# Moving four filter loads from SyncE's queue to GpSimd's

## The chip, the cores and the metric

The kernel runs on one core of a Trainium2 chip. The metric is the device time of one execution in microseconds; lower is better. A profile of one execution shows, beside its time, the span from the first to the last instruction and what every engine did in it: PE (TensorE matmuls; PEld is its weight loads), DVE (VectorE), ACT (ScalarE), POOL (GpSimd) and SP (SyncE, which here only issues transfers).

## What is computed

The input x is bf16, one sequence of 2048 positions with 512 channels. Two blocks follow each other, each with a residual.

```
x  = A_x                                              # 1 x 2048 x 512, bf16
h  = x + irfft2( rfft2(layernorm(x)) * (w_r + i*w_i) )  # over positions and channels
z  = layernorm(layernorm(h))                          # the second block normalizes twice
u  = gelu( einsum("bsd,sf->bdf", z, w1) + b1 )        # mixes positions, f = 1376
h2 = h + transpose( einsum("bdf,fs->bds", u, w2) + b2 )
```

w_r and w_i are 2048 x 257, bf16: the filter, a complex factor for every frequency. w1 is 2048 x 1376 and w2 is 1376 x 2048.

## The kernel before

**The Fourier transforms are matmuls with constant matrices.** The 2048 positions are split as 128 times 16, so a transform over positions is one stage of 128-point matrices (`A`, 16 of them, with the matrix F already scaled by each row's 1/standard deviation) and one of 16-point matrices (`C`). The 512 channels are transformed between them (`B`). After the filter the same comes back: `I`, `Bi` and `Ai`. The code keeps 16 chunks c of the spectrum, each holding two values of tau (2c and 2c + 1).

**One chunk's way through the middle of the kernel** is short, and the prediction follows it by these names:

- `B{c}` on PE, `Be{c}` empties its PSUM bank into a buffer (ACT or DVE);
- `C{c}` on PE, `Ce{c}` empties it into Xsb (a p behind the number means two chunks in one step);
- `P{c}` on DVE multiplies the spectrum by the filter: a tensor_tensor of Xsb and the tile W (line 674);
- `I{c}` on PE transforms back, `Ie{c}` empties it into TT (lines 708 and 709). `I{c}` uses PSUM bank 5 + c mod 3, so I10 needs the bank that Ie7 empties.

After the last chunk come `ID`, `Bi`, `Ai` (the rest of the inverse transform and the residual), the second block's norm, `m1` (line 844, matmul with w1), gelu (line 944) and `m2` (lines 962 and 968, matmul with w2), and the stores.

**Where the filter comes from.** The tile W holds 32 values of tau, for w_r (comp 0) and w_i (comp 1). It is loaded in three pieces of tau (line 510):

```
pieces = [(0, 8), (8, 18), (18, 32)]
```

Piece 0 serves P0 to P3, piece 1 P4 to P8, piece 2 P9 to P15. A load fills every fourth partition (32 of 128) with rows of 256 bf16 values, 512 bytes each, so piece 2 is eight loads of 32 x 14 rows, 224 KB each: four of w_r, then four of w_i. All loads of a piece count on one semaphore, and a P waits for the whole piece.

**The order of work.** A small planner, `schedule`, orders the instructions of each engine; for PE, ACT, DVE and POOL the beginning of the order is a list written out by hand, passed in `K.schedule`. SP has no list: it issues by the loads' `prio`, which is x and F first, then E, L and H, then W piece 0, 1 and 2 (`prio` 1.0, 2.0 and 3.0), then ID, GD and IF, then w1 and w2. `gen_sync` turns dependences into semaphore waits, and an engine runs its list strictly in order.

DVE's list in the stretch at hand is

```
P4 Be8 P5 Ie2_0 P7 P6 Ie4_0 P9 P8 Ie6_0 P10 P11 Ie7_0 P13 P12 Ie10_0 P14 P15 Ie14_0 Ie15_0
```

and PE's is

```
I4 B13 B12 C10p I6 I5 B14 C12p I7 B15 I8 I9 C14 I10 C15 I11 I12 I13 I14 I15 wmd ID00
```

POOL multiplies F by the row scales (`fs0` to `fs15`, line 577), then computes seven small vectors of negated means (`nm`, line 617, first read after the last chunk), then issues three small loads of the two bias vectors (`ld_b1a`, `ld_b2`, `ld_b1b`), each behind a wait for `Ye15`, the last emptying of stage A, and casts them to fp32 (lines 937 to 940).

Of the kernel before, what the change touches and what calls it, by code (L numbers as in the profile page):

```python
# [11 lines left out]
NP = 128  # L12
# [453 lines left out]
def build_kernel(nc, A_x, A_w_r, A_w_i, B_w1, B_b1, B_w2, B_b2, out, verbose=False):  # L466
# [10 lines left out]
    X, Y, FS, F, E, Lm, Hm, W, TT, GD, IF = (T[n] for n in ("X", "Y", "FS", "F", "E", "Lm", "Hm", "W", "TT", "GD", "IF"))  # L477
# [9 lines left out]
    def dma(name, q, dst, src, nbytes, prio=0.0, after=(), group=None, wgroup=None, store=False, land=None):  # L487
        def emit(e, eng):
            with nc.allow_non_contiguous_dma(reason="layout"):
                return eng.dma_start(dst, src)  # L490
        return K.op(name, q, emit, ins=[src] if store else [], outs=[] if store else [dst], occ=450.0, prio=prio,
                    after=after, nbytes=nbytes, group=group, wgroup=wgroup, land=land)
# [18 lines left out]
    for pi, (ta, tb) in enumerate(pieces):  # L511
        for comp, wsrc in enumerate((A_w_r, A_w_i)):
            wv = wsrc.rearrange("(q r) k -> q r k", r=64)
            for reim in range(2):
                parts = [(0, ta, tb, wv[:, ta:tb, 1:257])]
                lo = ta
                if ta == 0:
                    parts.append((1, 0, 1, wv[:, 32:33, 1:257]))
                    lo = 1
                parts.append((1, lo, tb, wv[:, 64 - lo:64 - tb:-1, 1:257]))  # L520
                for ss, a, b, src in parts:
                    dma(f"ld_w{comp}_{pi}_{reim}_{ss}_{a}", "sp", W[2 * ss + reim:NP:4, a:b, comp, :], src, 32 * 512 * (b - a),
                        prio=1.0 + pi, group=f"W{pi}", wgroup=f"W{pi}")

    K.op("mk_eps", "dve", lambda e, eng: eng.memset(eps[:, 0:1], LN_EPS), outs=[eps[:, 0:1]], occ=70.0, lat=130.0, prio=0)  # L525
    K.op("mk_eps2", "dve", lambda e, eng: eng.memset(eps[:, 1:2], LN_EPS * LN_EPS), outs=[eps[:, 1:2]], occ=70.0, lat=130.0, prio=0)
# [21 lines left out]
    for ga, gb in RS_GROUPS:  # L548
# [18 lines left out]
        for n2 in range(ga, gb):  # L567
            if n2 < NSPLIT:
                for sg in range(2):
# [4 lines left out]
                         prio=-5 + 0.1 * g)  # L574
# [380 lines left out]
    for n2 in range(NS2):  # L955
        b = 3 + n2 % 5
# [14 lines left out]
        else:  # L971
# [19 lines left out]
               "ag14 bn15 ag15 Ye6 Ye10 Ye14 Be2 Ce0 P0 P1 Ie0_0 P3 P2 Be7 P4 Be8 P5 Ie2_0 P7 P6 Ie4_0 P9 P8 Ie6_0 P10 P11 Ie7_0 P13 P12 "  # L991
               "Ie10_0 P14 P15 Ie14_0 Ie15_0 Bie01 bq01 bq00 aq0 sd2_1 sd2_0 hh00 hh01 h01 h00 hh1 h2 sd3_0 sd3_1 sd4_0 sd4_1 h3 sd5_1 hh2 "
               "sd5_0 h4 sd6_1 sd6_0 hh3 h5 sd7_1 hh4 h6 sd8_0 sd7_0 hh5 sd8_1 h7 sd9_1 hh6 sd9_0 h8 hh7 sd10_1 sd10_0 h9 hh8".split(),
        "pool": "fs1 fs0 fs2 fs4 fs5 fs3 fs6 fs7 fs8 fs9 fs12 fs10 fs11 fs13 fs14 fs15 nm2 nm7 nm3 nm4 nm0 nm1 nm8 ld_b1a ld_b2 ld_b1b b2f "
               "b1f_a b1f_b".split(),
    })
    K.gen_sync()
# [31 lines left out]
def bass_sequential_preLN__spectral_gfnet__mixer_token_mlp__prompt_kernel(  # L1029
    nc,  # L1030
    A_x,
    A_w_r,
    A_w_i,
    B_x,
    B_w1,
    B_b1,
    B_w2,
    B_b2,
    out,
):  # L1040
    build_kernel(nc, A_x, A_w_r, A_w_i, B_w1, B_b1, B_w2, B_b2, out)
# [28 lines left out]
```

## Time and profile before

| | |
|---|---|
| median of 7 runs | 130.81 us (130.15 to 132.22) |
| the profiled execution | 130.81 us, span 129.0 us |
| TensorE clock granted | 1.00 |
| busy: PE, DVE, ACT, POOL | 121.4, 65.1, 65.0, 11.8 us |
| read from HBM, written | 20.49 MB, 2.10 MB |

Busy time is the time in which an engine executes instructions; issuing a transfer is not counted in it, so SP has none. In timelines a line gives start and length in microseconds, the engine (SPq is SP's sequencer), the line of the kernel, the operation, what it writes and reads, and how many instructions are merged; in square brackets stands the idle time of the engine before it and who ended it. Instructions on one engine overlap a little: DVE's casts last 0.69 us each but follow each other every 0.61 us. Times of a view are counted from the start of the span.

### The profile page before, as it was taken

What the parts mean: (1) busy time and instruction counts of PE and PEld (TensorE: products, weight loads), DVE (VectorE), ACT (ScalarE), POOL (GpSimd) and SP (SyncE); (2) the same over time, 40 slices, a digit from 0 to 9 for tenths busy, and PEclk for the clock granted to TensorE, in tenths of its full rate; (3) what the DMA queues carried; (4) which work ended last, traced back from release to release, by engine and by line L of the source; (5) the groups of instructions that cost most, each with busy time, mean ns of one, the idle gap of its engine ahead of it and who ended that gap; (6) DMA issues with size and microseconds to landing.
All of it is one profiled execution on the core that took longest, in us unless ns stands there. A gap on an engine that the chain in (4) does not pass through costs nothing.

```text
span 129.0 us, 2036 instructions
## 1 busy us (share of the span) xinstructions
PE 121.4 (94%) x777; PEld 74.1 (57%) x786; DVE 65.1 (50%) x141; ACT 65.0 (50%) x137; POOL 11.8 (9%) x33
## 2 busy tenths in 40 slices
PE   6959979999899999999999999999999999999990
PEld 2337657777676655555544444456666666666660
DVE  1689949986978999968650000000422423323322
ACT  4688979999868999897777712222000000000000
POOL 0058980200000000000000000000000000000000
PEclk9999999999999999999999999999999999999999
DMA  3999998999999999999100000000112111121121
GB/s 71 371 395 380 242 219 169 277 319 363 396 425 425 415 416 422 244 390 400 42 0 0 0 0 5 0 0 0 41 49 73 41 67 60 41 81 41 41 84 41
DMA packets 16505, 22.71 MB, mean 176 GB/s; under 512 B 1552, under 2 KB 12304, under 8 KB 16368
## 3 DMA queue, kind: packets, MB, share of 16 engines
q1 hardware_dynamic: 15808, 21.66, 48.5%
q10 hardware_dynamic: 576, 0.92, 2.0%
q8 instruction: 6, 0.10, 0.3%
q0 software_dynamic: 112, 0.01, 0.3%
q14 instruction: 3, 0.02, 0.1%
HBM read 20.49 MB, written 2.10 MB: 175 GB/s over the span
## 4 chain that ended last, share of the span: by engine, by line
PE 71%; SPq 18%; DVE 3%; DMA 3%; issue 2%; DVEq 0%
PE ps L844 29%; PE ps L962 28%; SPq L490 18%; PE ps L771 5%; DMA W<-in_A_w_i_dram 3%; PE ps L692 3%; PE ps L808 2%; DVE P L674 2%; PE ps L968 2%; PE ps L911 1%; DVE TT L709 1%; DVE OUT L974 1%; PE ps L864 0%; PE ps L801 0%; PE ps L533 0%
## 5 line engine op out<-in xcount | busy, mean ns | idle before, releaser
L844 PE MATMUL ps<-HH,W 128*128 128x512 bf16 (+1 forms) x168 | 39.4, 379 | 0.2
L962 PE MATMUL ps<-GT,W 128*128 128x512 bf16 (+1 forms) x162 | 35.7, 379 | 0.2
L974 DVE SCALAR_TENSOR_TENSOR OUT<-ps,B2f,H 128x512 bf16<-128x512 f32 x16 | 12.0, 751 | 46.7 <-PE ps L962 24.4
L962 PEld LDWEIGHTS ps<-GT,W 128*128 128x128 bf16 (+1 forms) x165 | 23.7, 144 | 12.0
L844 PEld LDWEIGHTS ps<-HH,W 128*128 128x128 bf16 (+1 forms) x170 | 16.9, 100 | 17.6 <-issue 0.2
L944 ACT ACTIVATE GT<-ps,B1f 128x512 bf16<-128x512 f32 (+1 forms) x11 | 7.0, 691 | 12.7 <-PE ps L844 11.8
L818 DVE TENSOR_TENSOR H<-ps,X 128x512 bf16<-128x512 f32 x14 | 9.7, 691 | 4.0 <-PE ps L808 3.4
L824 ACT ACTIVATE SQ<-H,nm 128x512 bf16<-128x512 bf16 x14 | 10.1, 721 | 2.7 <-DVE H L818 2.4
L674 DVE TENSOR_TENSOR P<-Xsb,W 128x1024 bf16<-128x1024 bf16 x16 | 10.4, 685 | 1.6 <-DMA W<-in_A_w_i_dram 1.5
L559 DVE BATCH_NORM_STATS2 st<-X 128x6 f32<-128x512 bf16 x13 | 8.3, 679 | 3.6 <-DMA X<-in_A_x_dram 3.5
L593 PE MATMUL ps<-FS,X 128*128 128x256 bf16 x64 | 8.0, 273 | 1.7 <-POOL FS L577 1.6
L692 PE MATMUL ps<-Hm,P 128*128 128x128 bf16 x128 | 9.1, 220 | 0.5 <-DVE TT L709 0.4
L781 ACT ACTIVATE EO<-ps 128x512 bf16<-128x512 f32 x15 | 8.8, 586 | 0.9 <-PE ps L771 0.7
L637 PE MATMUL ps<-E,Y 128*128 128x256 bf16 x64 | 8.5, 273 | 0.7 <-ACT Y L607 0.7
L771 PE MATMUL ps<-GD,TT 128*128 128x256 bf16 x60 | 9.0, 273 | 0.1
L692 PEld LDWEIGHTS ps<-Hm,P 128*128 128x128 bf16 x128 | 7.4, 98 | 2.5 <-issue 1.3
L665 ACT ACTIVATE Xsb<-ps 128x1024 bf16<-128x1024 f32 (+1 forms) x9 | 8.0, 886 | 0.5 <-PE ps L652 0.4
L577 POOL TENSOR_SCALAR FS<-F,rs 128x256 bf16<-128x256 bf16 x16 | 7.4, 481 | 7.7 <-DMA F<-c_F 6.5
L641 ACT ACTIVATE Bsb<-ps 128x512 bf16<-128x512 f32 x13 | 7.3, 594 | 1.2 <-PE ps L637 1.2
L593 PEld LDWEIGHTS ps<-FS,X 128*128 128x128 bf16 x64 | 5.3, 97 | 4.5 <-POOL FS L577 3.0
L771 PEld LDWEIGHTS ps<-GD,TT 128*128 128x128 bf16 x60 | 5.8, 98 | 3.0 <-ACT EO L781 0.2
L533 PE MATMUL ps<-WM 128*128 128x512 bf16 (+1 forms) x19 | 6.2, 475 | 1.2 <-DVE eps L525 1.2
(70 smaller groups left out, 96.3 us busy)
## 6 DMA issues: line engine op xcount, KB each, us to landing
W<-in_B_w_dram SPq DMA_DIRECT2D x8, 688.0 KB, 11.7
W<-in_B_w_dram SPq DMA_DIRECT2D x10, 512.0 KB, 17.8
out_dram<-OUT SPq DMA_DIRECT2D x16, 128.0 KB, 1.7
X<-in_A_x_dram SPq DMA_DIRECT2D x4, 256.0 KB, 6.4
F<-c_F SPq DMA_DIRECT2D x4, 256.0 KB, 6.5
IF<-c_IF SPq DMA_DIRECT2D x1, 1024.0 KB, 7.2
W<-in_A_w_r_dram SPq DMA_DIRECT2D x4, 224.0 KB, 3.6
W<-in_A_w_i_dram SPq DMA_DIRECT2D x4, 224.0 KB, 3.8
```

Source lines behind the costliest of these rows:

```text
L490: return eng.dma_start(dst, src)
L593: r = eng.matmul(ps[:, b, 256 * u:256 * u + 256].rearrange("p (a b) -> p a b", a=2), X[:, n2, 128 * t:128 * t + 128], fr if t < 2 else fa, ...
L637: r = eng.matmul(o, Y[:, k, c, :], E[:, k, :].rearrange("p (h r) -> p h r", h=2), start=(i == 0), stop=(i == 3), skip_group_check=True)
L674: return eng.tensor_tensor(P[:, :, :, :], x.unsqueeze(2).broadcast_to([NP, 2, 2, 256]), W[:, 2 * c:2 * c + 2, :, :], ALU.mult)
L692: r = eng.matmul(o, P[:, h, m, par::2], Hm[:, v, m, :].rearrange("p (m r) -> p m r", r=4), start=(h == 0 and m == 0 and (par == 0 or b != ...
L771: r = eng.matmul(o, TT[:, q, n2, par, :], GD[:, par, q, :], start=(i == 0), stop=(i == 3), skip_group_check=True)
L781: return eng.activation(eo[:, :], ps[:, bE, :], ACT.Copy)
L818: K.op(f"h{n2}", "dve", lambda e, eng: eng.tensor_tensor(H[:, n2, :], ps[:, bA, :], X[:, n2, :], ALU.add), ins=[ps[:, bA, :], X[:, n2, :]] ...
L824: K.op(f"sq{n2}", "act", lambda e, eng: eng.activation(sq[:, :], hsrc, ACT.Square, bias=nm[:, n2, 0:1], accum_out=s2t[:, n2, 0:1]), ins=[h ...
L844: return eng.matmul(ps[0:Mt, bank, :], W1[:, n2, 128 * t:128 * t + Mt], HH[:, n2, :], start=(n2 == 0), stop=(n2 == 15), skip_group_check=True)
L962: r = eng.matmul(ps[:, b, :], W2[t][0:Kt, n2::16], GT[0:Kt, t, :], start=(t == 0), stop=(t == NFT - 1), skip_group_check=True)
L974: K.op(f"fin{n2}", "dve", lambda e, eng, n2=n2, b=b: eng.scalar_tensor_tensor(OUT[:, n2, :], ps[:, b, :], B2f[:, n2:n2 + 1], H[:, n2, :], ...
```

## The change

The four w_i loads of piece 2 are issued by POOL instead of SP. In POOL's list they stand right behind `fs15`, the last scaling of F, and ahead of the `nm` vectors and the bias loads. Piece 2 gets two semaphores (groups W20 and W21), one for w_r and one for w_i; the other two pieces keep one (W00 and W10, new names only). P9 and the P behind it need both. What is loaded, and where to, stays the same.

```diff
                 for ss, a, b, src in parts:
-                    dma(f"ld_w{comp}_{pi}_{reim}_{ss}_{a}", "sp", W[2 * ss + reim:NP:4, a:b, comp, :], src, 32 * 512 * (b - a),
-                        prio=1.0 + pi, group=f"W{pi}", wgroup=f"W{pi}")
+                    dma(f"ld_w{comp}_{pi}_{reim}_{ss}_{a}", "pool" if (comp, pi) == (1, 2) else "sp", W[2 * ss + reim:NP:4, a:b, comp, :], src, 32 * 512 * (b - a),
+                        prio=1.0 + pi, group=f"W{pi}{comp * (pi == 2)}", wgroup=f"W{pi}")
...
-        "pool": "fs1 fs0 fs2 fs4 fs5 fs3 fs6 fs7 fs8 fs9 fs12 fs10 fs11 fs13 fs14 fs15 nm2 nm7 nm3 nm4 nm0 nm1 nm8 ld_b1a ld_b2 ld_b1b b2f "
+        "pool": "fs1 fs0 fs2 fs4 fs5 fs3 fs6 fs7 fs8 fs9 fs12 fs10 fs11 fs13 fs14 fs15 ld_w1_2_0_0_18 ld_w1_2_0_1_18 ld_w1_2_1_0_18 ld_w1_2_1_1_18 nm2 nm7 nm3 nm4 nm0 nm1 nm8 ld_b1a ld_b2 ld_b1b b2f "
                 "b1f_a b1f_b".split(),
```

## The prediction

> **What bounds the kernel now.** I began with the page's chain of work that ended last, then read that chain in order of time, then the timelines of the queues that feed its one visible stall. The page's totals first:
>
> ```profile
> PE 71%; SPq 18%; DVE 3%; DMA 3%; issue 2%; DVEq 0%
> L674 DVE TENSOR_TENSOR P<-Xsb,W 128x1024 bf16<-128x1024 bf16 x16 | 10.4, 685 | 1.6 <-DMA W<-in_A_w_i_dram 1.5
> ```
>
> SPq's 18% is not a busy engine: it is the first 26 us, in which SP issues load after load with 0.04 us between them and the last load of the filter comes out at the end of the row. The second line says what that costs: of all 16 filter products, one waited, for 1.5 us. The chain in order of time (start, length, what) shows the place:
>
> ```profile
> 25.20 0.63 SPq L490
> ...
> 25.88 4.28 DMA W<-in_A_w_i_dram
> ...
> 30.25 1.29 DVE P L674 x2
> 31.54 0.60 DVE TT L709
> 32.15 1.20 DVE P L674 x2
> 33.35 0.61 DVE TT L709
> 33.96 0.05 issue
> 34.00 0.62 PE ps L692 x8
> ```
>
> The last load of piece 2 is issued at 25.88 and lands at 30.16; P9 and P8 start at 30.25. In the DVE's timeline the instruction before them, Ie4_0, starts at 28.02 and DVE issues its casts 0.61 us apart, so P9 could have come at 28.63: 1.62 us. After 34.00 the chain is PE to the end, with DVE's share 1% and no DMA. Whatever reaches PE at 34 to 37.7 us reaches the end.
>
> SP's own timeline, and POOL's, from which the change borrows:
>
> ```profile
> 17.41 3.75 SPq L490 DMA_DIRECT2D W<-in_A_w_i_dram  x4
> 21.19 2.63 SPq L490 DMA_DIRECT2D W<-in_A_w_r_dram  x4
> 23.86 2.64 SPq L490 DMA_DIRECT2D W<-in_A_w_i_dram  x4
> 26.55 0.61 SPq L490 DMA_DIRECT2D ID<-c_ID  x1
> 12.82 2.76 POOL L577 TENSOR_SCALAR FS<-F,rs 128x256 bf16<-128x256 bf16 x6 [0.29 <-ACT rs L565]
> 15.55 0.23 POOL L617 TENSOR_SCALAR nm<-mv 128x1 f32<-128x1 f32 x1
> 17.40 1.18 POOL L490 DMA_DIRECT2D B1s<-in_B_b_dram  x1
> 18.58 0.56 POOL L490 DMA_DIRECT2D B2s<-in_B_b_dram  x1
> 23.41 0.54 POOL L490 DMA_DIRECT2D B1s<-in_B_b_dram  x1 [4.28 <-DMA B1s<-in_B_b_dram]
> ```
>
> A load of piece 2 costs SP 0.67 us. POOL is done with FS at 15.55, 8.3 us before SP comes to the four loads that move (23.86). The last question is whether the DMA engines have room between 17 and 24 us (busy times of PE, PEld, DVE, ACT, POOL, then granted clock, DMA share, GB/s):
>
> ```profile
> 17.60:19.60 2.00, 2.00 (x23) 1.37 (x21) 0.99 (x2) 1.72 (x4) 1.54 (x2) 1.00 0.97 243
> 19.60:21.20 1.60, 1.60 (x21) 1.10 (x20) 1.49 (x3) 1.60 (x4) 0.00 (x0) 1.00 0.62 117
> 21.20:24.20 3.00, 3.00 (x42) 2.39 (x40) 2.65 (x5) 2.95 (x5) 0.75 (x2) 1.00 1.01 241
> 26.50:30.25 3.75, 3.75 (x53) 2.79 (x51) 2.14 (x5) 3.75 (x7) 0.26 (x2) 1.00 1.14 341
> ```
>
> 341 GB/s is reached at 26.5 to 30.25, so 243, 117 and 241 is what SP hands out, not what the engines can take. The shares near 1 beside those rates are the reason for doubt.
>
> **The change, part by part.**
>
> *Removed from SP:* four issues, 4 x 0.67 = 2.67 us. ID, GD, IF, W1 and W2 are issued that much earlier. That is worth nothing: no wait of PE, ACT or DVE after 30.25 is for a DMA. For the same reason it costs nothing.
>
> *Added to POOL:* four issues of 448 rows of 512 B. The trace shows POOL issues of 96 elements (0.54 us) and of 1280 (1.18 us). The straight line between gives 0.54 + 352 x 0.64/1184 = 0.73 us; bounds 0.54 and 1.18. Four take 2.9 us (2.2 to 4.7), from 15.55 to 18.5, the last issued at 17.7 (17.2 to 19.1). POOL's loads landed 3.0 to 5.7 us after issue, with little data; 0.92 MB at 341 GB/s is 2.7 us more if all of it queues. So the last lands between 20.2 and 19.1 + 5.7 + 2.7 = 27.5; I take 24. It is needed at 28.63, so it is in time at both ends.
>
> *Left on SP:* the w_r half of piece 2 keeps its issue times. Its last issue at 23.19 lands 3.7 later by the DMA view, at 26.9, 1.7 us before it is needed.
>
> *Queued behind on POOL:* nm (15.55), the bias loads (17.40) and their casts (26.44) move 2.9 us back. nm is first read at 41.0, the biases by the first gelu at 69.6: free, with over 20 us of cover. The 1280-element load then runs beside the w_r half of piece 2 rather than beside piece 1.
>
> *Added wait:* piece 2 now has two semaphores, so P9 waits once more. Such a step is 0.02 to 0.06 us in the chain before P9; it lies within the slack below.
>
> *What the stall's removal is worth.* Not 1.62. I move the rows by their own spacings. P9 28.63, P8 29.24. Ie6_0 needs I6 on PE (29.34) and comes 0.66 us after it, as Ie4_0 (28.02) comes after I4 (27.36): 30.00. P10 needs Ce10p, which ACT ends at 29.50 + 1.02 = 30.52: 30.6; P11 31.2. Ie7_0 needs I7 (31.32): 31.98, not 33.26. P13 needs Ce12p (31.58 + 1.02 = 32.60): 32.65; P12 33.26. Now PE:
>
> ```profile
> 33.20 0.39 PE L652 MATMUL ps<-Bsb,Lm 64*128 64x256 bf16 x4
> 34.00 0.62 PE L692 MATMUL ps<-Hm,P 128*128 128x128 bf16 x8 [0.41 <-DVE TT L709]
> 34.56 0.39 PE L652 MATMUL ps<-Bsb,Lm 64*128 64x256 bf16 x4
> ```
>
> These are C14, I10, C15. PE ran without a gap from 28.8 to C14, so C14 stays at 33.20. I10 waited for Ie7_0, which empties its bank; freed, it follows C14 by 0.32 (as I11 at 34.88 follows C15), at 33.52. Ie10_0 0.66 later, 34.18; P14 0.61 later, 34.79, against 35.67 in the profile. Ce15 keeps up (C15 at 34.08, Ce15 34.5 to 35.1, before P15 at 35.4). So the train arrives 35.67 - 34.79 = **0.88 us** earlier: PE's own work and ACT's Ce12p are next in line and eat the other 0.74. From 37.7 on everything shifts by 0.88.
>
> *The sum:* the profiled execution has a span of 129.0 and a time of 130.81, which is also the median of the seven runs; 1.81 lies around the span. 129.0 - 0.88 + 1.81 = **129.93 us**.
>
> *What speaks against it on piece 1.* P4 starts at 24.25; the last load of piece 1, issued at 20.53, landed 3.6 later, at 24.15. It has 0.1 us, and POOL's 0.92 MB come just before it. But the new train has slack: P9's is 28.63 - 28.48 = 0.15, Ie6_0's wait for I6 adds 0.15, Ie7_0's 0.17, P13's 0.07, Ie10_0's (33.26 + 0.61 = 33.87 against 34.18) 0.31. So 0.85 us of delay at P4 costs nothing and each us beyond costs one. Bounds: between 17.6 and 24.2 the engines move 243 x 2.0 + 117 x 1.6 + 241 x 3.0 = 1.40 MB, and at 341 GB/s could move 2.25, so 0.85 of the 0.92 MB fits into the holes: delay 0.2 us. With none of the holes used, 2.7. I take 0.2 to 0.8, nearer the rates shown.
>
> The Trainium skill's "DMA: Bandwidth & Descriptors", section "Rules for kernel authors", speaks against the change: issuing from several engines brings no bandwidth, since all run on the same DMA engines, and saves issue time alone. Here SP's issue is what runs solid and the rate is under its later 341 GB/s, so the rule leaves room; were the engines full, the sum would be 130.8. "SBUF — State Buffer", section "SBUF: two separate sides", warns that a GpSimd DMA is starved of descriptors during some VectorE instructions, about 3100 ns in place of 620; an estimate from it is landings near 31 us and no gain. In 15.5 to 20.1 VectorE here only empties PSUM; no run shows such starving yet.
>
> **The rivals.** *A, the bursts collide (slower).* POOL's loads are served first, piece 1 lands late, and P4 stalls. For: the 0.1 us of slack, DMA shares of 0.97 and 1.01, and SP's issue at 18.73 that took 1.76 us. Against: the hole of 117 GB/s. Price: 2.7 - 0.85 - 0.88 = 0.97 us slower, 131.8; if SP's long issue doubles its extra 1.1 us as well, 132.9. It decides from piece 1 landing past 24.15 + 0.1 + 0.85 + 0.88 = 26.0.
>
> *B, the wait remains.* POOL's issues cost over 3 us each, or w_r is dragged to 30; P9 still waits for a W. For: no POOL load of this shape in the trace. Against: 1280 elements took 1.18. Price: 130.0 to 131.5, about 130.8.
>
> *C, all of it comes through.* PE and ACT follow DVE more closely than I moved them: 130.81 - 1.53 = 129.3. Against: PE shows no gap from 28.8 to 33.6.
>
> **How the numbers follow.** Forecast 0.62, A 0.13, B 0.14, C 0.11. The predicted time is the forecast's, 129.9. Runs of this kernel spread from 130.15 to 132.22, and 1% (1.3 us) is about what a measurement tells from no change. The range goes from C, 129.2, to halfway into A, 131.3. Faster by over 1% (under 129.5): C and a little of the forecast, 0.16. Slower by over 1% (over 132.1): A where it runs on past its lower price, and the slow end of B, 0.12. Within 1%: 0.72.
>
> **What would show it.** P9 at 28.6 to 28.7 after Ie4_0, no DVE wait on W; POOL's four issues at 15.55 with 0.5 to 1.2 us each; ID's issue at 23.9; I10 near 33.5 with no wait on DVE TT; the first ID matmul (37.97) near 37.1. I am wrong if P4 moves past 25.1, if a W wait stands before P9, or if P14 moves by less than 0.5.

## The result, and the profile after

The change makes the kernel slower. Its median is 131.46 us (27 runs, 131.19 to 133.58) against 130.68 us (64 runs of the kernel before): a ratio of 1.0071, 95% interval 1.0055 to 1.0086. Some executions of these kernels fall into a slower state; they stay in the medians and ranges given here and below, while the ratios leave them out. The forecast was 129.93, and 131.46 lies 0.16 past the end of its range. The profiled execution took 131.29 us with a span of 129.5, against 130.81 and 129.0, so 0.5 us of the loss can be read in the two traces.

The wait that the change was aimed at is gone, but the group of the 16 filter products still waits. The page of after has these two lines, first the shares of the chain that ended last:

```profile
PE 84%; DMA 5%; ACT 5%; DVE 3%; issue 1%; ACTq 1%; POOL 0%
...
L674 DVE TENSOR_TENSOR P<-Xsb,W 128x1024 bf16<-128x1024 bf16 x16 | 10.4, 684 | 2.3 <-ACT Xsb L665 2.2
```

2.2 us in place of 1.5, and for something else. (That the chain has no SPq any more, where before had 18%, proves nothing: at the one wait left it follows the wrong releaser, as shown below.) In the DVE's timeline of before, P4 and, later, P14 are these lines:

```profile
24.25 0.69 DVE L674 TENSOR_TENSOR P<-Xsb,W 128x1024 bf16<-128x1024 bf16 x1
...
35.67 1.28 DVE L674 TENSOR_TENSOR P<-Xsb,W 128x1024 bf16<-128x1024 bf16 x2
```

The DVE's timeline of after shows where the new wait is:

```profile
23.40 0.69 DVE L642 CAST Bsb<-ps 128x512 bf16<-128x512 f32 x1 [0.15 <-PE ps L637]
26.31 0.69 DVE L674 TENSOR_TENSOR P<-Xsb,W 128x1024 bf16<-128x1024 bf16 x1 [2.22 <-ACT Xsb L665]
...
29.92 0.68 DVE L709 CAST TT<-ps 128x512 bf16<-128x512 f32 x1
30.52 1.28 DVE L674 TENSOR_TENSOR P<-Xsb,W 128x1024 bf16<-128x1024 bf16 x2
...
36.17 1.28 DVE L674 TENSOR_TENSOR P<-Xsb,W 128x1024 bf16<-128x1024 bf16 x2
```

P9 and P8 (30.52) follow Ie4_0 without a gap: no wait for piece 2 is left. The new wait stands before P4, at 26.31 in place of 24.25. The releaser in the brackets is a neighbour that happened to end at 26.29: that ACT instruction (25.27 to 26.29) empties a later chunk, and the one that P4 reads had ended at 23.88. What P4 waited for is piece 1. Its last load, issued by SP at 19.75, takes this long to land in the DMA view of that one issue:

```profile
W<-in_A_w_i_dram SPq DMA_DIRECT2D x1, 160.0 KB, 6.5
```

19.75 + 6.5 is 26.2, and the piece's semaphore is complete at 26.22; before, the same load landed 3.6 us after its issue, at 24.15. Not all of these 2.07 us are the change's: in this execution SP reached its first load of piece 1 at 15.07 and not at 14.76, 0.31 us later, and it was late by as much at its first filter load (7.13 against 6.82), before any load that the change moved. The last P pair ahead of the long PE stretch, P14, moves from 35.67 to 36.17, by the 0.5 us of the span.

SP's and POOL's timelines of after show that the issues themselves went as planned:

```profile
15.07 2.60 SPq L490 DMA_DIRECT2D W<-in_A_w_r_dram  x4
17.70 2.79 SPq L490 DMA_DIRECT2D W<-in_A_w_i_dram  x4
20.53 3.85 SPq L490 DMA_DIRECT2D W<-in_A_w_r_dram  x4
24.43 1.38 SPq L490 DMA_DIRECT2D ID<-c_ID  x1
...
15.29 2.73 POOL L490 DMA_DIRECT2D W<-in_A_w_i_dram  x4
...
19.93 1.01 POOL L490 DMA_DIRECT2D B1s<-in_B_b_dram  x1
20.95 0.57 POOL L490 DMA_DIRECT2D B2s<-in_B_b_dram  x1
```

POOL needs 2.73 us for its four, and they have all landed by 23.14. Their packets run from 17.2 to 22.7 us, so in that stretch piece 2's w_i half is in the DMA engines together with piece 1, which is needed 4 us sooner. The table of windows (columns as in the prediction) for the same stretches, and the one behind them:

```profile
17.60:19.60 2.00, 2.00 (x23) 1.37 (x21) 1.23 (x2) 1.78 (x4) 1.65 (x7) 1.00 1.02 323
19.60:21.20 1.60, 1.60 (x22) 1.06 (x20) 1.45 (x3) 1.60 (x4) 1.52 (x4) 1.00 1.08 343
21.20:24.20 3.00, 3.00 (x41) 2.42 (x39) 2.58 (x4) 2.96 (x5) 0.32 (x1) 1.00 1.08 307
24.20:26.20 2.00, 2.00 (x25) 1.25 (x22) 0.00 (x0) 1.73 (x3) 0.31 (x1) 1.00 1.16 244
```

The holes of before (243, 117, 241 GB/s) are filled: 323 x 2.0 + 343 x 1.6 + 307 x 3.0 is 2.12 MB, 0.72 MB more than before. But whose bytes? The share of the queues in 18 to 22 us (packets, MB, share of the 16 engines; q1 is SP's, q0 POOL's), first before:

```profile
q1 hardware_dynamic: 1428, 0.70, 72.1%
q0 software_dynamic: 78, 0.01, 8.5%
```

and after:

```profile
q0 software_dynamic: 293, 0.83, 60.1%
q1 hardware_dynamic: 977, 0.48, 40.9%
```

POOL's 0.83 MB came in, and SP's queue, which carries piece 1, fell from 0.70 to 0.48 MB.

### The profile page after: what moved, and what is told of

The parts are those of the page before. It is cut to its first block, busy times and chain, and to the rows that moved or that the text cites. A ratio compares the mean times of both kernels' runs of the same rounds, so it can differ in the third digit from the quotient of the medians.

```text
span 129.5 us, 2036 instructions
## 1 busy us (share of the span) xinstructions
PE 121.5 (94%) x777; PEld 74.3 (57%) x786; DVE 65.1 (50%) x141; ACT 65.1 (50%) x137; POOL 14.8 (11%) x37
## 3 DMA queue, kind: packets, MB, share of 16 engines
HBM read 20.49 MB, written 2.10 MB: 174 GB/s over the span
## 4 chain that ended last, share of the span: by engine, by line
PE 84%; DMA 5%; ACT 5%; DVE 3%; issue 1%; ACTq 1%; POOL 0%
PE ps L844 29%; PE ps L962 27%; PE ps L692 6%; PE ps L637 6%; PE ps L771 5%; DMA X<-in_A_x_dram 5%; PE ps L652 3%; ACT Y L607 3%; PE ps L808 2%; PE ps L968 2%; PE ps L593 2%; PE ps L911 1%; DVE st L559 1%; ACT Xsb L665 1%; ACTq L490 1%
## 5 line engine op out<-in xcount | busy, mean ns | idle before, releaser
L533 PE MATMUL ps<-WM 128*128 128x512 bf16 (+1 forms) x19 | 6.7, 504 | 1.2 <-DVE eps L525 1.2
L637 PEld LDWEIGHTS ps<-E,Y 128*128 128x128 bf16 x64 | 5.6, 98 | 3.7 <-DVE Bsb L642 1.9
## 6 DMA issues: line engine op xcount, KB each, us to landing
W<-in_B_w_dram SPq DMA_DIRECT2D x10, 512.0 KB, 17.2
```

The source lines that it names most:

```text
L637: r = eng.matmul(o, Y[:, k, c, :], E[:, k, :].rearrange("p (h r) -> p h r", h=2), start=(i == 0), stop=(i == 3), skip_group_check=True)
```

## The experiments

Times are medians, ratios are to the kernel before on the same chip, with a 95% interval. "P4", "P9" and "P14" are the starts of these instructions in the profile.

**e1: no wait for piece 2 at all.** The kernel before, in which the four loads do not exist; P9 to P15 multiply with the w_r half of the filter twice, so the w_i half of piece 2 is left out of the computation. It prices the wait alone.

```diff
-                for ss, a, b, src in parts:
+                for ss, a, b, src in ([] if (comp, pi) == (1, 2) else parts):
...
-  ... W[:, 2 * c:2 * c + 2, :, :], ALU.mult)
+  ... W[:, 2 * c:2 * c + 2, :, :] if c < 9 else W[:, 2 * c:2 * c + 2, 0:1, :].broadcast_to([NP, 2, 2, 256]), ALU.mult)
```

> The kernel before, with the four w_i loads of piece 2 left out altogether; P9 to P15 multiply by the w_r half twice (same shapes, same instruction). Nothing is put on POOL. This prices the removed stall by itself. If the step of the prediction that turned a 1.62 us stall into 0.88 us is right: no DVE wait on W before P9, P14 about 0.9 us earlier, 129.8 us (129.5 to 130.1). Rival: the stall was cover for something else and its removal is worth nothing, 130.5 to 130.8; or all of it counts, 129.1.

Measured: 129.80 us, ratio 0.993 (0.9898 to 0.9962). The DVE's timeline of e1, with P4, P9 and P14:

```profile
24.48 0.68 DVE L674 TENSOR_TENSOR P<-Xsb,W 128x1024 bf16<-128x1024 bf16 x1
...
28.86 1.28 DVE L674 TENSOR_TENSOR P<-Xsb,W 128x1024 bf16<-128x1024 bf16 x2
...
35.02 1.28 DVE L674 TENSOR_TENSOR P<-Xsb,W 128x1024 bf16<-128x1024 bf16 x2
```

The wait is worth 0.84 us by the medians (130.64 - 129.80) and 0.9 by the ratio, whose interval goes from 0.5 to 1.3 us: about the prediction's 0.88, and not its length of 1.5. From P4 to P14 an undisturbed train takes 35.02 - 24.48 = 10.54 us, where the kernel before took 35.67 - 24.25 = 11.42: 0.88 more.

**e2 and e3: the bias loads later.** POOL's three bias loads wait for Ie15_0, behind the last filter product; in e2 on the changed kernel, in e3 on the kernel before.

```diff
-    dma("ld_b1a", "pool", B1s[:, 0:10], ..., 2560, prio=20, after=gate)
+    dma("ld_b1a", "pool", B1s[:, 0:10], ..., 2560, prio=20, after=[o for o in K.ops if o.name == "Ie15_0"])
...
```

> The changed kernel, with the three bias loads of POOL held back until the middle stage is over (they wait for Ie15_0, near 38 us). Theory: piece 1 is late for two reasons, POOL's filter packets taking the DMA engines between 17 and 22 us, and the 1280 two-byte rows of the bias load, whose packets now run at 23.6 to 24.7 us, just where the last load of piece 1 lands. If the bias load holds about half of the 2.06 us, P4 starts near 25.3 and the time is 130.4 (130.0 to 130.8), with SP's long issue at 21.3 gone. Rival: POOL's filter loads alone do it, P4 stays at 26.0 or later and the time at 131.3.

> The kernel before, with the three bias loads held back until Ie15_0; the filter loads stay on SP. If the bias load with its two-byte rows is what makes one SP issue last 1.76 us, that issue becomes 0.62, piece 2 lands 1.1 us earlier, P9 waits 0.4 and the time is 130.1 (129.9 to 130.4). Rival: the long issue belongs to the 16 KB instruction fetch that runs at the same time; then nothing moves and the time is 130.7.

Measured: e2 130.59 us, ratio 0.9985 (0.9959 to 1.001); e3 130.89, ratio 1.0013 (0.9983 to 1.0044). The DVE's timeline of e2:

```profile
25.66 0.69 DVE L674 TENSOR_TENSOR P<-Xsb,W 128x1024 bf16<-128x1024 bf16 x1 [1.57 <-DMA W<-in_A_w_i_dram]
...
29.87 1.28 DVE L674 TENSOR_TENSOR P<-Xsb,W 128x1024 bf16<-128x1024 bf16 x2
...
35.52 1.28 DVE L674 TENSOR_TENSOR P<-Xsb,W 128x1024 bf16<-128x1024 bf16 x2
```

Here the releaser of P4 is named as what it is, a load of w_i. P4 is 0.65 us earlier than in the changed kernel but still 1.41 later than in the kernel before. The time is 0.87 below the changed kernel's by the medians and 1.1 by the ratios, 0.66 by the two profiled executions. So the bias loads, which the change pushed from 17.40 to 19.93 and onto piece 1's last load, are a part of the loss; the larger part of piece 1's delay stays. How large their part is remains open: of the 0.65 at P4, 0.30 is again that SP began piece 1 earlier in this execution (14.77). SP's long issue, which I had expected to go with them, stayed (1.93 us at 21.42). In the kernel before the same edit brings nothing, as nobody waits there. Its P4 and P9:

```profile
24.32 0.68 DVE L674 TENSOR_TENSOR P<-Xsb,W 128x1024 bf16<-128x1024 bf16 x1
...
30.28 1.29 DVE L674 TENSOR_TENSOR P<-Xsb,W 128x1024 bf16<-128x1024 bf16 x2 [1.49 <-DMA W<-in_A_w_i_dram]
```

**e4: POOL's loads held back.** The four loads stand behind nm and wait for P1, so that piece 1 goes first.

```diff
-  (POOL's list) ... fs15 ld_w1_2_0_0_18 ld_w1_2_0_1_18 ld_w1_2_1_0_18 ld_w1_2_1_1_18 nm2 ... nm8 ld_b1a ...
+  (POOL's list) ... fs15 nm2 ... nm8 ld_w1_2_0_0_18 ld_w1_2_0_1_18 ld_w1_2_1_0_18 ld_w1_2_1_1_18 ld_b1a ...
+  (the four loads) after=[P1]
```

> The changed kernel, with POOL's four filter loads held back until P1 is done (near 21.2 us), behind the nm vectors and still ahead of the bias loads. Their packets then start near 23, when nearly all of piece 1 is through. Theory: what was lost is the place of the loads, not that POOL issues them. P4 goes back to 24.0 to 24.5, P9 starts between 28.6 and 29.6, time 130.1 (129.7 to 130.6). Rival: POOL's loads cost time wherever they stand, because they push out the w_r half of piece 2 or because SP's later loads come earlier; then 131.0 or more.

Measured: 131.47 us, ratio 1.0053 (1.0025 to 1.0081). My expectation failed. POOL's timeline of e4, and then the DVE's:

```profile
21.35 2.73 POOL L490 DMA_DIRECT2D W<-in_A_w_i_dram  x4 [4.25 <-DVE P L674]
24.07 0.95 POOL L490 DMA_DIRECT2D B1s<-in_B_b_dram  x1
```

```profile
23.89 0.68 DVE L674 TENSOR_TENSOR P<-Xsb,W 128x1024 bf16<-128x1024 bf16 x1
...
30.94 1.29 DVE L674 TENSOR_TENSOR P<-Xsb,W 128x1024 bf16<-128x1024 bf16 x2 [2.58 <-DMA W<-in_A_w_r_dram]
```

P4 is early again: with POOL's bytes, and the bias loads behind them, out of its way, piece 1 is in time. But now both halves of piece 2 arrive late: w_i at 29.56 and, last, w_r, SP's half, at 30.86, 2.5 us after P9 could have started (30.94 - 2.58 = 28.36). At either place the load of SP's that lies beside POOL's loads comes late. Here the bias loads lie beside it too, so e4 does not say how much is the four loads' alone.

**e5 and e6: the other four loads on POOL.** Piece 1's w_i half is issued by POOL, all of piece 2 by SP; e6 has the bias loads late as well. If issue time was the gain and the order of bytes the loss, this takes the one without the other: the bytes that overtake are now the ones needed first.

```diff
-  "pool" if (comp, pi) == (1, 2) else "sp"    ... group=f"W{pi}{comp * (pi == 2)}"
+  "pool" if (comp, pi) == (1, 1) else "sp"    ... group=f"W{pi}{comp * (pi == 1)}"
-  (POOL's list) ... fs15 ld_w1_2_0_0_18 ld_w1_2_0_1_18 ld_w1_2_1_0_18 ld_w1_2_1_1_18 nm2 ...
+  (POOL's list) ... fs15 ld_w1_1_0_0_8 ld_w1_1_0_1_8 ld_w1_1_1_0_8 ld_w1_1_1_1_8 nm2 ...
```

> As many loads on POOL, at the same place in its list, but the four w_i loads of piece 1 (160 KB each) in place of those of piece 2. SP issues the w_r half of piece 1, then all of piece 2. If POOL's 4096-byte packets push SP's 512-byte ones aside, POOL is the right queue for what is needed first: piece 1's w_i lands near 22, its w_r near 22 to 23, P4 stays at 24.0 to 24.4; piece 2 leaves SP at 22.8 and lands near 27.5, P9 without a W wait at 28.5: 129.9 us (129.6 to 130.4). Rival: what costs is the amount that POOL moves, whoever needs it; then P4 is late again and the time is 131 or more.

> The kernel e5_piece1_pool with the bias loads held back until Ie15_0. The bias load's two-byte rows then meet neither piece. If they only matter where a filter load has no slack, this is the same as e5_piece1_pool, 129.8 to 129.9; if they slow piece 2 past 28.5, it is 0.3 to 0.8 us faster than e5_piece1_pool.

Measured: e5 129.68 us, ratio 0.9944 (0.9919 to 0.9968); e6 129.69, ratio 0.9943 (0.9918 to 0.9969). Both beat the kernel before and the changed one, and lie where e1 lies, which had no wait. The DVE's timeline of e5:

```profile
23.98 0.68 DVE L674 TENSOR_TENSOR P<-Xsb,W 128x1024 bf16<-128x1024 bf16 x1
...
29.34 1.29 DVE L674 TENSOR_TENSOR P<-Xsb,W 128x1024 bf16<-128x1024 bf16 x2 [0.88 <-ACT Bsb L641]
...
34.76 1.28 DVE L674 TENSOR_TENSOR P<-Xsb,W 128x1024 bf16<-128x1024 bf16 x2
```

Against my expectation P9 still waits 0.88 (piece 2 is complete at 29.25; the bracket again names a neighbour): SP began the w_i half of piece 2 at 20.52 in place of 23.86, but its four issues took twice as long.

```profile
20.52 5.14 SPq L490 DMA_DIRECT2D W<-in_A_w_i_dram  x4
```

In e6, where P9 starts at 28.43 without a wait, P14 is only 0.21 earlier, at 34.55. A wait of 0.9 at P9 is thus almost free.

**e7 and e8: two loads instead of four.** POOL issues only half of piece 2's w_i (0.46 MB); e8 has the bias loads late.

```diff
-  "pool" if (comp, pi) == (1, 2) else "sp"
+  "pool" if (comp, pi, reim) == (1, 2, 1) else "sp"
-  (POOL's list) ... fs15 ld_w1_2_0_0_18 ld_w1_2_0_1_18 ld_w1_2_1_0_18 ld_w1_2_1_1_18 nm2 ...
+  (POOL's list) ... fs15 ld_w1_2_1_0_18 ld_w1_2_1_1_18 nm2 ...
```

> The changed kernel with two of the four loads on POOL (the second half of piece 2's w_i) and the other two still on SP behind w_r. Half the burst: POOL moves 0.46 MB before piece 1 is through. If the delay of piece 1 goes with the bytes that POOL moves, P4 starts near 25.2 (half of 2.06 us late), which is just about the slack of 0.85 us; SP's last filter load is issued 1.3 us earlier, P9 near 29.2; 130.3 us (129.9 to 130.7). Rival: the delay is a step that any POOL load causes, then P4 is near 26.3 and the time near 131.4.

> The kernel e7_two_pool with the bias loads held back until Ie15_0. With half the burst and no bias load, P4 is late by 0.3 to 0.8 us, within the slack, P9 near 28.7 to 29.0: 129.9 us (129.7 to 130.3). If the bias load does nothing here, the same as e7_two_pool.

Measured: e7 130.35 us, ratio 0.9989 (0.9966 to 1.0011); e8 129.84, ratio 0.9945 (0.9921 to 0.997). P4 in the DVE's timeline of e7, and then of e8:

```profile
25.79 0.69 DVE L674 TENSOR_TENSOR P<-Xsb,W 128x1024 bf16<-128x1024 bf16 x1 [1.67 <-DMA W<-in_A_w_i_dram]
```

```profile
24.19 0.69 DVE L674 TENSOR_TENSOR P<-Xsb,W 128x1024 bf16<-128x1024 bf16 x1
```

With half the bytes and no bias load piece 1 is in time, and the time is that of e5 and e1. With the bias load P4 is 1.6 us late in the profiled execution (which, at 130.84, is the slowest of e7's twelve) and the median loses 0.51. What the two causes do to piece 1 can be read from the time between SP's first issue of it and its complete landing (the last update of its semaphore), one execution a cell:

| POOL's filter bytes ahead of it | bias loads late | bias loads early |
|---|---|---|
| none | 8.38 (e3) | 9.40 (before) |
| 0.46 MB | 9.28 (e8) | 11.05 (e7) |
| 0.92 MB | 10.79 (e2) | 11.15 (after) |

Down the column without the bias load: 0.9 us for the first 0.46 MB, 1.5 for the second. Across: 1.02, 1.77 and 0.36 for the bias loads. The two do not simply add.

The first row also holds something that the others do not. There one of SP's issues took 1.66 or 1.76 us, so that SP's last issue of the piece came 5.7 or 5.8 us after the first, in the other rows 4.7 to 4.9. What that is worth can be seen in e1, whose loads up to piece 1 are those of before: there the last issue came 4.6 us after the first, and the piece took 9.10 us in place of 9.40. So without the long issue the first row would be some 0.2 to 0.3 us lower, and POOL's first 0.46 MB would cost that much more; this is an estimate from that one pair. How far two executions of one kernel differ in this time was not measured, so the 0.36 alone shows little.

**e9: the same loads from ACT's queue.** POOL's queue moves its rows in packets of 4096 and 2048 bytes, SP's in packets of 512. If the larger packets were what gave POOL its lead, the same loads in packets of 512 should leave piece 1 alone. In e9 ACT issues the four behind Ye7; the bias loads are late as in e2. ACT's own work is held up by the issues, so the time (132.91, one run) says nothing on the question, and only the transfers are read.

```diff
-  "pool" if (comp, pi) == (1, 2) else "sp"
+  "act" if (comp, pi) == (1, 2) else "sp"
+  (ACT's list) ... Ye7 ld_w1_2_0_0_18 ld_w1_2_0_1_18 ld_w1_2_1_0_18 ld_w1_2_1_1_18 Ye12 ...
```

> The kernel e2_after_bias_late, with the four w_i loads of piece 2 issued by ACT instead of POOL at about the same time (behind Ye7, near 15.3 us), so in packets of 512 bytes like SP's. ACT loses 2.5 us by issuing them, so the total time says nothing (near 133 us) and only the transfers are read. If POOL's loads win because a packet of theirs is 4096 bytes against SP's 512, then with equal packets the two queues share equally: over the four us in which both have work SP's queue gets at least half of 1.3 MB (0.65 MB, not 0.55), and piece 1 lands before 25.0 (25.6 with POOL). If it is the bytes alone, piece 1 lands at 25.5 or later again.

Measured: piece 1 took 10.40 us by the count of the table, against 10.79 in e2 and 8.38 without other loads; it landed at 25.33, between my two bounds. The queues in 17 to 21 us of e9 (q10 is ACT's), in which ACT's loads overtake just as POOL's did:

```profile
q10 hardware_dynamic: 1410, 0.70, 63.3%
q1 hardware_dynamic: 1097, 0.53, 45.8%
```

Most of the delay is there with equal packets, so it comes from the bytes that go first. Whether the size of the packets accounts for the remaining 0.4 us stays open, since ACT's loads also started 1.1 us earlier than POOL's, and both are single executions.

## Why the prediction was wrong, point by point

- **POOL's issues and landing: right.** 2.73 us for four where 2.9 was taken (0.85 for the first, then 0.63 to 0.64), all landed at 23.14 where 24 was taken. The Trainium skill ("SBUF — State Buffer", section "SBUF: two separate sides") warns that a GpSimd DMA is starved of descriptors beside some VectorE instructions, 3.1 us in place of 0.62. That did not show here: each issue took 0.63 to 0.85 us beside VectorE's casts out of PSUM, and in e4 the four took 2.73 again beside two filter products, which read SBUF.
- **The wait at P9: right.** No wait is left there, and P9 follows Ie4_0 directly, though at 30.52 and not at 28.63.
- **What its removal is worth, 0.88 and not 1.62: right**, by e1 (0.84 by the medians, 0.88 from P4 to P14) and by e5 and e6, in which 0.9 us of waiting at P9 moves P14 by 0.21.
- **The delay of piece 1: wrong, and this is the step that failed.** The prediction saw the danger (0.1 us of slack at P4, bounds of 0.2 and 2.7 us) and took "0.2 to 0.8, nearer the rates shown". At P4 it was 2.06, or 1.75 by the table, without SP's own later start. The reckoning behind it asked how much of POOL's 0.92 MB fits into the holes of the DMA engines, and that part came out nearly right: 0.72 MB more were moved by 24.2, where 0.85 had been said to fit. What it left out is the order. The two queues shared the engines; the later-needed bytes went through by 23.14, and the shortfall of 0.2 MB fell on SP's queue, where piece 1 stands. Even so, 0.2 MB at 341 GB/s would be only 0.6 us, so bytes alone do not give the delay. SP's queue had finished as many 512-byte rows as pieces 0 and 1 hold (4608) at 24.25, where before it had at 23.12: 1.13 us later. But the piece was complete only 2.0 us after that count, where before it was 1.0. As a piece is complete soon after its last row (before, piece 2 was at 30.16, its last row at 29.84), rows of piece 2 must have gone ahead of the last rows of piece 1 within SP's own queue, more of them in the changed kernel. Why was not tested. The tests of the cause as a whole are e2, e4 and e8: move the bias loads alone and P4 stays late, at 25.66; hold POOL's bytes back as well and it starts at 23.89; halve them (and move the bias loads) and it starts at 24.19.
- **The bias load "then runs beside the w_r half of piece 2 rather than beside piece 1": wrong.** It was filed under free, looking only at who reads the biases. At 19.93 it met piece 1's last load, issued at 19.75. Taking the bias loads away again shortens piece 1 by 0.36 us in the profiled executions, brings P4 forward by 0.65 and the time by 0.9 to 1.1 (e2).
- **The w_r half of piece 2, said to land at 26.9: wrong, but hidden.** It landed at 28.71, 0.08 us past the 28.63 at which P9 had been forecast; P9 came later than that for piece 1's sake.
- **ID's issue at 23.9: 24.43**, since SP's four w_r issues of piece 2 took 3.85 us in place of 2.63. It costs nothing, as predicted: nobody waits for it.
- **The slack of 0.85 at P4: somewhat too large.** From P4 to P14 the changed kernel takes 36.17 - 26.31 = 9.86 us, e2 the same, against 10.54 undisturbed in e1: 0.68.

With the two measured terms in the prediction's own sum, 129.93 + 2.06 - 0.68 = 131.31, against 131.29 in the profiled execution. Both terms are read from that same execution, so the agreement shows only that all that lies behind P14 moves with it; that the median, 131.46, is as near is in part luck, as the 0.31 us of SP's later start stands in the 2.06. The mechanism is that of rival A, which was to decide from piece 1 landing past 26.0; it landed at 26.22. A's price of 131.8 took the full bound of 2.7.

The Trainium skill's "DMA: Bandwidth & Descriptors", section "Rules for kernel authors", says that issuing from several engines brings no bandwidth and saves issue time only. The windows agree: the rate rose to 323, 343 and 307 GB/s, to about the 341 that SP's loads alone had reached later in the kernel before, and hardly past it. The time saved at issue is real, and e5 turns it into 0.56%; what the change added is that the saved time went to the wrong bytes.

## What to carry to other kernels

When loads move to a second queue they do not only start sooner: they go ahead of, or beside, whatever the first queue still has to deliver. Price the delay of the first queue's next deadline by the bytes that overtake it, not by the free bandwidth on average; and if something has to overtake, let it be what is needed first. Small loads that slide along behind the moved ones need the same question: beside whose last bytes will they land?

## What the runs showed of the hardware that I had not expected

- **Two small loads can cost more than their bytes.** The bias loads of 1280 elements of 2 bytes (2.5 KB) and, right behind it, of 4 KB sent their packets at 23.7 to 24.6 us in the changed kernel; the rate in 24 to 25.25 us fell to 174 GB/s, from over 300 in the stretch before, and with these loads moved away (e2) it is 287 there. By the table they lengthen piece 1 by 0.36 to 1.77 us. Which of the two does it was not tested.
- **POOL's issue time grows little with rows.** 448 rows of 512 bytes took 0.63 us, where 96 elements had taken 0.54: a straight line to the 1.18 us of 1280 elements gave 0.73. In e5, 320 rows took 0.60.
- **SP's long issue is not the bias load's doing.** I had suspected it of the 1.76 us issue at 18.73. In e3, without a bias load at that time, SP's timeline has the four issues of piece 1's w_i at nearly the same length, the third of them 1.66 us long:

```profile
17.59 3.65 SPq L490 DMA_DIRECT2D W<-in_A_w_i_dram  x4
```

  In before, e1, e3 and e4 such a long issue (0.93 us in e1) ends 0.36 to 0.41 us after a 16 KB packet of the instruction queue (q8) has ended, for instance 20.49 after 20.09. In the changed kernel the long issue (21.32 to 23.03) does not go with such a packet, and neither does the one of e2 (21.42 to 23.34). That the fetch causes the others was not tested, and what held up these is open.
